# GpSimd strips kept off VectorE's composite passes, the last copy in two tiles, and a new table of turns in an attention and feed-forward kernel

## The chip, the cores and the metric

The kernel runs on one core of a Trainium2 chip. A core has five engines with a queue each: TensorE (PE, with a separate row for its weight loads, PEld), VectorE (DVE), ScalarE (ACT), GpSimd (POOL) and SyncE (SP, here only a queue of DMAs). The metric is the device time of one execution in microseconds (us); the time of a kernel is the median of several executions.

## The reference

Both branches read the same `x` of 2048 rows by 512 columns in bfloat16, and a gate mixes them:

```python
g = _sigmoid((x * gate_w).sum(-1, keepdims=True))
a = _A_ref(x, A_wqkv, A_wo)                    # attention, 32 heads of 16 columns
b = _B_ref(x, B_w_gate, B_w_up, B_w_down)      # (silu(x @ w_gate) * (x @ w_up)) @ w_down, 1792 wide
return g * a + (1 - g) * b
```

In the attention, each head has scores of 2048 by 2048, `softmax(q k / 4)`, times `v`; the heads' results go through `wo`.

## The kernel before

**Tiling.** The attention is cut into 32 *units*: 4 blocks of 512 queries (`QBW`) times 8 groups of 4 heads. A unit has 16 *slots*, one for each block of 128 keys, so there are 512 slots. In a slot TensorE makes the scores of 4 heads, 128 keys by 512 queries each.

**Two ways to the exponential.** Most slots take ScalarE: two heads' scores (`s_t`, 128x1024 in PSUM) go through one `Exp` into `e_t` (`emit_pair`, line 752), two such pairs a slot. The rest take VectorE (`emit_d`, line 830): it reads one head's scores (`d_t`, 128x512) with a multiply and an add into 16-bit integers that stand for the bits of a rough exponential (line 848), four reads to a block of 128x2048, and then makes the value better with *passes* over the whole block (`class Pass`, line 882): either three shifted copies, so that TensorE sums four versions, or two bit masks and a product. `v_unit` (line 1607) decides when a block goes to VectorE, by the time that the plan expects VectorE to be free.

**Strips.** GpSimd helps with the passes (copies and products). `strip` (line 940) gives it the last columns of a pass, as many as fit into a time; `g_now` (line 979) works out this time: from the end of GpSimd's last strip, or 0.1 us after VectorE's last SBUF pass, to the end of the reads of PSUM that VectorE is expected to do next, plus `G_OVER` = 0.05 us (or 0.4 in turns marked `q`). The idea is that GpSimd works while VectorE reads PSUM. `wide(cost)` (line 339) tells which of the small waiting operations count as SBUF passes rather than as reads; it goes by their booked cost, under 0.45 us. Those, and the passes, are booked no earlier than the end of the running strip (`plan.lock`). A strip gets a semaphore on VectorE's last pass (`beside`, line 959).

**The plan.** All engines' queues are written in an order worked out in Python while the kernel is built. `plan` (line 318) holds a clock for each engine, with booked costs: 0.217 us for a matmul of 512 columns, 0.9167 for an exp tile, 0.6 for a read of PSUM and for a full copy pass, 1.135 for a product (`MUL_US`). `fill_dve` (line 1009) picks VectorE's next work; operations with a due time wait in `owed` (`later`, line 348) with a cost and, where given, a key. Where an operation has the key of the one just before it, `spend_v` adds 0.13 us and `fill_dve` looks for another that is due first. `TURNS` (line 87) holds two letters for each pair of score tiles; a letter changes one choice of the plan at that pair (how much slack a piece of work may take, whether a block may start, whether products or copies go to GpSimd, and others), and a dot changes nothing.

**The other work** is cut into pieces that the pacer puts into gaps of TensorE: the projections of q, k and v, the feed-forward chunks (56 of them: `gu_chain`, line 686), the down projections and the output. A chunk has `gate`, whose `Tanh` on ScalarE is followed on VectorE by `gs` (line 701), and `gated`, which multiplies by the up half into `mt` (line 689). `gate_end` (line 646) makes the odds of the gate for all rows at once, five small operations booked at 1.7; `recip` (line 1150) inverts a query block's softmax denominators and spreads them (`rn`, booked at 1.1 or 0.87).

**The end.** The last unit's result `o_ps` is copied to SBUF in two halves, one on VectorE and one on ScalarE (`post`, line 1123), both into one tile `osb`. Then `denominators` (four small matmuls into `dt`), a reciprocal (`rt`), `spread_rows` (16 small matmuls into `rps`), four products (`on_l`), four closing matmuls into `a_ps` (`a_l_a`, `a_l_b`, `al`, `al_o`), four evictions and the stores follow (lines 1757 to 1784). `rest` holds ten products of rows 2 and 3 of the last block that need none of this; `tail(n)` (line 1215) emits n of them.

Of the kernel before, what the change touches and what calls it, by code (L numbers as in the profile page):

```python
# [8 lines left out]
ACT = mybir.ActivationFunctionType  # L9
ALU = mybir.AluOpType  # L10
# [43 lines left out]
class Pacer:  # L54
# [30 lines left out]


TURNS = (
    "....d...sq.t.......q................i......v...........ld..q...........y........................"
    "...........n...............r......e............................................................."
    ".................................l........e.......................j..g...........v...m.....gk..."  # L90
    "..............o.......c...j........n..........h....l.......................t........k...b......."
    "..c.i......q....j.......c......u.........q..............................o......................."
    ".................................x...qh.....k.......................a..n...................u...l"
    "...........x..j.d..x.....x..a...........c.......j.c..wi...iw.................t....jv............"
    ".....t...v..k.c.a..l.rh.......j.h.......e.........on..i...............j......f............c...sy"
    "........kx..............j...............k...s...........................................a......f"
    "..c...................................................................o....uj......x............"
    "..c...d..q.q.....y...uh.d............ra.................k.b......n............i.a..fe..........."
    ".....................................................................................m.......x.q"
    ".......tkq...vb....l.............y..b..u...y.................qe........n...x..e.............e..q"  # L100
    "........b........................vc....l...............g.l..d............f.......y.g..k........q"
    "................................................b..........m..............h....................."
    "........k................n.....ya"
)


# [1 line left out]
def kernel(  # L108
# [13 lines left out]
    P = 128  # L122
# [71 lines left out]
    def act(*args, **kw):  # L194
        ordered(nc.scalar.activation(*args, **kw))  # L195
# [136 lines left out]
    def spend(mode, mms, ready=0.0):  # L332
# [3 lines left out]
        plan.pe = max(plan.pe + (FLIP if mode != plan.mode else 0.0), ready) + (0.226 if mode == "F" else 0.217) * mms  # L336
        plan.mode = mode

    def wide(cost):
        return cost < 0.45  # L340

    def took():
        plan.alone, plan.alone_ins = plan.dve, last_of.get(nc.vector.engine)
# [342 lines left out]
    def gu_chain(i):  # L686

        def gated(up):
            vec.scalar_tensor_tensor(out=mt[:, FS[i][1], :], in0=gs_of.pop(i)[:], scalar=0.5, in1=up[:, :],
                                     op0=ALU.mult, op1=ALU.mult)  # L690
            m_free(up, plan.dve)

        def gate(gp):
            th = work.tile([P, QBW], BF16, tag="th", name="th")
            flush_act(plan.pe + 0.5)
            act(out=th[:], in_=gp[:, :], func=ACT.Tanh, scale=0.5)
            plan.act = max(plan.act, plan.pe + 0.38) + 0.49

            def f():
                gs = work.tile([P, QBW], BF16, tag="gs", name="gs")  # L700
                vec.scalar_tensor_tensor(out=gs[:], in0=th[:], scalar=1.0, in1=gp[:, :], op0=ALU.add, op1=ALU.mult)
                m_free(gp, plan.dve)
                gs_of[i] = gs
            gs_at[i] = plan.act + 0.05
            later(0.6, f, gs_at[i])

        cs = slice(FS[i][0] * QBW, (FS[i][0] + 1) * QBW)
        return [columns(DC, "gu", lambda dc, w=w: w[i][:, dc, :], lambda dc: xT[:, dc, cs], end)
                for w, end in ((w_gate, gate), (w_up, lambda p: later(0.6, lambda: gated(p), max(plan.pe + 0.25, gs_at[i]))))]

    scaled = set()

# [251 lines left out]

    G_FIX, G_COPY, G_PRODUCT = 0.195, 0.00083, 0.00187
    G_LEAST, G_LEAVE = 192, 160
    G_OVER = 0.05
    MASKS = False

    def claim(now):  # L970
# [8 lines left out]
    def g_now(now):  # L979

        while True:
            g = claim(now)
            if g is None:
                return
            start = max(plan.pool, plan.alone + 0.1, g.ready + 0.1, 0.0 if g.c is not None or not g.home else min(c_free) + 0.1)
            t = now
            for ready, cost in sorted([(d[0], 0.6) for d in d_wait] + [(o[0], o[1]) for o in owed if not wide(o[1])]):
                if ready > t + 0.05:
                    break
                t += cost  # L990
            if t == now or not g.strip(start, t + (G_OVER if way_of(pairs[0]) != "q" else 0.4) - start):
                return
# [129 lines left out]

    def post(un):
        qb, g = UNIT[un]
        osbs[un] = osb0[qb] if g == 0 else work.tile([P, QBW], BF16, tag="osb", name="osb")
        if un == 0:
            assert part_scaled
            vec.scalar_tensor_tensor(out=osbs[un][:, :], in0=o_of.pop(un)[:, :], scalar=tiny[:, 0:1], in1=o_part, op0=ALU.add, op1=ALU.add)
        elif un == UNITS - 1:
            o, hw = o_of.pop(un), QBW // 2  # L1130
            vec.tensor_scalar(out=osbs[un][:, 0:hw], in0=o[:, 0:hw], scalar1=tiny[:, 0:1], scalar2=None, op0=ALU.add)
            act(out=osbs[un][:, hw:], in_=o[:, hw:], func=ACT.Identity, bias=tiny[:, 0:1], scale=1.0)
        else:
            vec.tensor_scalar(out=osbs[un][:, :], in0=o_of.pop(un)[:, :], scalar1=tiny[:, 0:1], scalar2=None, op0=ALU.add)

# [14 lines left out]
    def recip(qb, g1, n0):  # L1150

        n = 4 * g1
        dn = work.tile([P, P], BF16, tag="dn", name="dn")
        queue.dma_start(out=dn[0:4 * n, :], in_=dds[qb][0:n, :].rearrange("h (a c) -> (h a) c", c=P))
        full = qb < QB - 1
        if full:
            rd = work.tile([P, QBW], BF16, tag="rd", name="rd")[:, :].bitcast(F32)
            queue.dma_start(out=rd[:, 0:P], in_=odds_rows[0][TQ * qb:TQ * (qb + 1), :].unsqueeze(0).broadcast_to([H, TQ, P]))

        def spread():  # L1160
            rn = work.tile([P, P], BF16, tag="rn", name="rn")
            if full:
                vec.reciprocal(rd[:, P:2 * P], dn[:, :])
                vec.tensor_tensor(out=rn[:, :], in0=rd[:, P:2 * P], in1=rd[:, 0:P], op=ALU.mult)
            else:
                recip16(rn[0:4 * n, :], dn[0:4 * n, :])
            rr = dram.tile([H, QBW], BF16, tag="rr", name="rr")
            queue.dma_start(out=rr[0:n, :].rearrange("h (a c) -> (h a) c", c=P), in_=rn[0:4 * n, :])
            for b in range(g1 // 2):
                queue.dma_start(out=rb[:, b, :],  # L1170
                                  in_=rr[8 * b:8 * b + 8, :].unsqueeze(1).broadcast_to([8, DH, QBW]))
        at.setdefault(n0 + 6, []).append(lambda: later(1.1 if full else 0.87, spread))
        for b in range(g1 // 2):
            def norm(b=b):
                vec.tensor_tensor(out=onc[qb][:, b, :], in0=onc[qb][:, b, :], in1=rb[:, b, :], op=ALU.mult)
                normed.add((qb, b))
            at.setdefault(n0 + 13 + b, []).append(lambda norm=norm: later(0.345, norm))

    def denominators(p, osb):
        for tq in range(TQ):  # L1180
            mm(p[:, 4 * tq:4 * tq + 4], lhsT=osb[:, tq * P:(tq + 1) * P], rhs=sel_t[:, :], start=True, stop=True)

    def spread_rows(p, rt):
        for tq in range(TQ):
# [583 lines left out]
    on_l = work.tile([P, QBW], BF16, tag="rd", name="on_l")  # L1768
    for tq in range(TQ):
        cs = slice(tq * P, (tq + 1) * P)  # L1770
        vec.tensor_tensor(out=on_l[:, cs], in0=osb[:, cs], in1=rps[:, cs], op=ALU.mult)
# [44 lines left out]
```

## Time and profile before

| | before |
|---|---|
| time, median of 3 | 754.49 us (753.93 to 754.78) |
| the profiled execution | 753.96 us |
| its span in the profile | 752.2 us |
| granted TensorE clock | 1.00 |
| VectorE reads of score tiles into `c_t` | 460, mean 679 ns |
| ScalarE exp tiles | 756, mean 1071 ns |
| GpSimd strips of copies within `c_t` | 173, mean 789 ns |

The span is shorter than the time by what lies around the program on the device. The profile names a group of instructions by line, engine, operation, what it writes and reads (`c_t<-d_t`), shape and count; behind the bar stand its busy time, the mean of one and the idle time before them. Lines are those of the helpers through which every operation goes, L192, L195 and L204, so the names of the tiles tell operations apart. In a timeline a row has start, length, engine and instruction; `x3` are three in a row. The reported spans of neighbours on VectorE and ScalarE overlap, so what an operation costs is the distance from its start to the next start.

### The profile page before, as it was taken

To read this page: it belongs to the slowest core of one execution; us is meant where nothing else is said; L and a number is where in the kernel's file an instruction comes from. 1 tells how busy PE (TensorE), PEld (TensorE's weight loads), DVE (VectorE), ACT (ScalarE), POOL (GpSimd) and SP (SyncE) were. 2 spreads that over 40 slices of the span, in tenths; PEclk is the share of its full clock that TensorE was granted. 3 is DMA by queue.
4 is the path that set the end of the run, shared out by engine and by line. 5 is a ranking of instruction groups with operands and counts; after the bars stand their busy time and mean duration, and the time that the engine had idled before them with its cause. 6 is when DMAs were issued, how large, how long until landed. Compare 5 with 4: busy or idle time off the path is not lost.

```text
span 752.2 us, 22877 instructions
## 1 busy us (share of the span) xinstructions
PE 731.6 (97%) x9213; PEld 215.6 (29%) x9213; DVE 728.6 (97%) x1233; ACT 733.4 (98%) x825; POOL 291.9 (39%) x352
## 2 busy tenths in 40 slices
PE   8999999999999999999999999999999999999997
PEld 3322222222222223222222222232222322232222
DVE  7899999999999999999999999999999999999994
ACT  5999999999999999999999999999999999999996
POOL 5125444334335353443532254532423363143430
PEclk9999999999999999999999999999999999999999
DMA  9000303153300013221100130311000232100001
GB/s 227 6 1 16 71 17 67 46 135 75 72 20 13 18 42 81 56 48 30 37 20 26 44 84 21 77 37 44 17 13 26 62 84 55 31 20 12 15 31 36
DMA packets 91027, 34.45 MB, mean 46 GB/s; under 512 B 75488, under 2 KB 90472, under 8 KB 90920
## 3 DMA queue, kind: packets, MB, share of 16 engines
q1 hardware_dynamic: 89192, 32.66, 18.1%
q8 instruction: 72, 1.18, 0.6%
q10 hardware_dynamic: 1728, 0.33, 0.2%
q14 instruction: 35, 0.29, 0.1%
HBM read 21.55 MB, written 2.35 MB: 32 GB/s over the span
## 4 chain that ended last, share of the span: by engine, by line
PE 57%; DVE 22%; ACT 14%; issue 5%; POOL 1%; DMA 0%; DVEq 0%; ACTq 0%; POOLq 0%
PE s_t L192 19%; PE o_ps L192 17%; DVE c_t L204 14%; ACT e_t L195 13%; PE gu L192 7%; PE ops L192 5%; PE qp L192 2%; PE kp L192 2%; PE vp L192 2%; DVE mt L204 2%; DVE kaug L204 2%; ACT th L195 1%; DVE gs L204 1%; DVE osb L204 1%; PE dps L192 1%
## 5 line engine op out<-in xcount | busy, mean ns | idle before, releaser
L195 ACT ACTIVATE e_t<-s_t 128x1024 bf16<-128x1024 f32 x756 | 707.7, 1071 | 4.5 <-PE d_t L192 1.7
L204 DVE TENSOR_SCALAR c_t<-d_t 128x512 uint16<-128x512 f32 x460 | 299.7, 679 | 2.1 <-PE d_t L192 1.8
L192 PE MATMUL s_t<-qx,kaug 32*128 32x512 bf16 (+1 forms) x1192 | 231.7, 384 | 7.6 <-ACT e_t L195 6.7
L204 POOL TENSOR_SCALAR c_t<-c_t 128x416 uint16<-128x416 uint16 (+19 forms) x173 | 136.6, 789 | 208.4 <-DVE c_t L204 154.8
L192 PEld LDWEIGHTS <-kaug 32*128 32x128 bf16 (+1 forms) x2048 | 79.3, 91 | 304.9 <-issue 301.6
L192 PE MATMUL d_t<-qx,kaug 32*128 32x512 bf16 x440 | 151.7, 383 | 0.6 <-DVE qx L204 0.3
L192 PE MATMUL o_ps<-e_t,vaug 128*32 128x512 bf16 (+2 forms) x1568 | 148.0, 378 | 0.0
L192 PE MATMUL o_ps<-c_t,vaug 128*32 128x512 bf16 (+2 forms) x1392 | 123.3, 372 | 1.4 <-POOL c_t L204 0.8
L204 DVE TENSOR_SCALAR c_t<-c_t 128x2048 uint16<-128x2048 uint16 (+3 forms) x187 | 121.8, 662 | 0.3
L204 POOL TENSOR_TENSOR c_t<-c_t 128x480 bf16<-128x480 bf16 (+13 forms) x60 | 65.2, 1103 | 131.9 <-DVE c_t L204 84.5
L192 PEld LDWEIGHTS <-vaug 128*32 128x32 bf16 x3216 | 70.5, 95 | 113.2 <-issue 100.6
L192 PE MATMUL gu<-xT,wg 128*32 128x512 bf16 x896 | 72.3, 383 | 0.4 <-DVE mt L204 0.2
L192 PE MATMUL gu<-xT,wu 128*32 128x512 bf16 x896 | 68.3, 382 | 0.3
L192 PE MATMUL ops<-wd_t,mt 128*32 128x512 bf16 x672 | 57.0, 382 | 0.0
L204 DVE TENSOR_TENSOR c_t<-c_t 128x2048 bf16<-128x2048 bf16 (+15 forms) x57 | 56.9, 998 | 0.0
L204 DVE TENSOR_SCALAR kaug<-d_t 128x512 uint16<-128x512 f32 x72 | 47.0, 680 | 0.6 <-PE d_t L192 0.6
L204 DVE SCALAR_TENSOR_TENSOR mt<-gs,gu 128x512 bf16<-128x512 bf16 x56 | 38.0, 679 | 1.6
L204 DVE SCALAR_TENSOR_TENSOR gs<-th,gu 128x512 bf16<-128x512 bf16 x56 | 37.8, 675 | 0.1
L192 PE MATMUL s_t<-q,kaug 32*128 32x512 bf16 (+1 forms) x188 | 36.6, 385 | 1.1 <-ACT e_t L195 0.9
L195 ACT ACTIVATE th<-gu 128x512 bf16<-128x512 f32 x56 | 35.8, 639 | 0.0
L204 POOL TENSOR_SCALAR kaug<-c_t 128x416 uint16<-128x416 uint16 (+15 forms) x34 | 26.8, 788 | 22.2 <-DVE c_t L204 20.0
L204 POOL TENSOR_SCALAR c_t<-kaug 128x1120 uint16<-128x1120 uint16 (+8 forms) x33 | 24.8, 753 | 23.1 <-DVE c_t L204 13.8
(149 smaller groups left out, 548.6 us busy)
## 6 DMA issues: line engine op xcount, KB each, us to landing
wg<-in_B_w_gate_dram SPq DMA_DIRECT2D x56, 128.0 KB
wu<-in_B_w_up_dram SPq DMA_DIRECT2D x56, 128.0 KB
on<-osb SPq DMA_DIRECT2D x120, 16.0 KB
rb<-rr SPq DMA_DIRECT2D x15, 128.0 KB
wd_t<-in_B_w_down_dram SPq DMA_DIRECT2D x7, 256.0 KB
qx<-qst SPq DMA_DIRECT2D x96, 16.0 KB
qx<-aq SPq DMA_DIRECT2D x96, 16.0 KB
out_dram<-o_t SPq DMA_DIRECT2D x12, 128.0 KB
```

What stands on the lines that cost most here:

```text
L192: return ordered(nc.tensor.matmul(*args, **kw))
L195: ordered(nc.scalar.activation(*args, **kw))
L204: return lambda *a, **kw: ordered(f(*a, **kw))
```

## The change

Seven edits in one:

- `wide` also holds for operations booked at 0.87, 1.4 or 1.7 us: the odds (`gate_end`) and the spread of reciprocals (`recip`), whose full form is now booked at 1.4 rather than 1.1. They are so kept from strips like the passes.
- `G_OVER` goes from 0.05 to 0: a strip ends, by the plan, with the last read. A strip behind another is booked to start 0.08 us after it.
- `gs` and the `mt` product of one chunk share a key.
- The two halves of the last copy get a tile each; `block` finds the columns of a row block in either form.
- The ten last products are put 3, 3, 2 and 2 instead of 2, 2 and 6, the last two between the second and the third closing matmul.
- In the evictions at the end, ScalarE takes the first and third, VectorE the second and fourth.
- `TURNS` is replaced: 150 letters before, 131 after, at other places.

```diff
 TURNS = (
-    "....d...sq.t.......q................i......v...........ld..q...........y........................"
...
+    "..........s...j.....d........................r.......................q....b...s......l.........l"
...
 )
+    PASSES = (0.87, 1.4, 1.7)
+
     def wide(cost):
-        return cost < 0.45
+        return cost < 0.45 or cost in PASSES
...
-            later(0.6, f, gs_at[i])
+            later(0.6, f, gs_at[i], ("g", i))
...
-                for w, end in ((w_gate, gate), (w_up, lambda p: later(0.6, lambda: gated(p), max(plan.pe + 0.25, gs_at[i]))))]
+                for w, end in ((w_gate, gate), (w_up, lambda p: later(0.6, lambda: gated(p), max(plan.pe + 0.25, gs_at[i]), ("g", i))))]
...
-    G_OVER = 0.05
+    G_OVER = 0.0
...
-            start = max(plan.pool, plan.alone + 0.1, g.ready + 0.1, 0.0 if g.c is not None or not g.home else min(c_free) + 0.1)
+            start = max(plan.pool + 0.08, plan.alone + 0.1, g.ready + 0.1, 0.0 if g.c is not None or not g.home else min(c_free) + 0.1)
...
-        osbs[un] = osb0[qb] if g == 0 else work.tile([P, QBW], BF16, tag="osb", name="osb")
+        if un < UNITS - 1:
+            osbs[un] = osb0[qb] if g == 0 else work.tile([P, QBW], BF16, tag="osb", name="osb")
...
-            vec.tensor_scalar(out=osbs[un][:, 0:hw], in0=o[:, 0:hw], scalar1=tiny[:, 0:1], scalar2=None, op0=ALU.add)
-            act(out=osbs[un][:, hw:], in_=o[:, hw:], func=ACT.Identity, bias=tiny[:, 0:1], scale=1.0)
+            osbs[un] = [work.tile([P, hw], BF16, tag=t, name="osb")[:, :] for t in ("osb", "th")]
+            vec.tensor_scalar(out=osbs[un][0], in0=o[:, 0:hw], scalar1=tiny[:, 0:1], scalar2=None, op0=ALU.add)
+            act(out=osbs[un][1], in_=o[:, hw:], func=ACT.Identity, bias=tiny[:, 0:1], scale=1.0)
...
-        at.setdefault(n0 + 6, []).append(lambda: later(1.1 if full else 0.87, spread))
+        at.setdefault(n0 + 6, []).append(lambda: later(1.4 if full else 0.87, spread))
...
+    def block(osb, tq):
+        if isinstance(osb, list):
+            osb, tq = osb[tq // 2], tq % 2
+        return osb[:, tq * P:(tq + 1) * P]
...
-    tail(min(2, len(rest)))
+    tail(min(3, len(rest)))
     dt = m_tile("dt")
     denominators(dt, osb)
...
-    tail(min(2, len(rest)))
+    tail(min(3, len(rest)))
...
     spread_rows(rps, rt)
-    tail(len(rest))
+    tail(min(2, len(rest)))
...
     for tq in range(TQ):
+        if tq == 2:
+            tail(len(rest))
         mm(a_ps[tq][:, 0:D], lhsT=on_l[:, tq * P:(tq + 1) * P], rhs=wo_l[:, 1, :], start=False, stop=True,
...
-        if tq % 2 == 0:
+        if tq % 2:
             vec.tensor_scalar(out=mt[:, tq, :], in0=a_ps[tq][:, 0:D], scalar1=gval[:, t:t + 1], scalar2=None, op0=ALU.mult)
```

More of the change, by code (lines that the diff above doesn't have):

```diff
@@ L87 @@
 TURNS = (
-    "....d...sq.t.......q................i......v...........ld..q...........y........................"
[L89 to L102, printed above, removed]
@@ L103 @@
-    "........k................n.....ya"
+    "..........s...j.....d........................r.......................q....b...s......l.........l"
+    ".....n.y...f.x....a...b.................k........t............k...h........x...........g....a.s."
+    ".......................t..................k...................o................................."
+    "...r......k....................n...................q.....g................k..............r.m...."
+    ".........w....................hq..........h...................o......y....d..n..k.....h........."
@@ new lines @@
+    "..hqj....xkt.y............a.c.....k....x....c.................................s...........o...j."
+    ".......t....j.......i....x......c.s.......e.............j......................................."
+    ".....q........................b..f......k.a...b....................................l............"
+    "..............o...................................s............................................."
+    "..........s........................r..............................................i.........j..."
@@ new lines @@
+    "..i............r..............................i............................r.....v........b....."
+    ".....q...g..c...b.........h......n...ye..q...q...lc........w............a....w......iq.........."
+    "..........b....................n..if.......t....c.............................d..............q.."
+    "...............f.......v....h......u....k..m..cxk........v..................................e..."
+    "...f..........j....q..................................o............w............kg.............."
@@ L104 @@
+    ".......g..................o"
 )
@@ L1177, in recip @@
             at.setdefault(n0 + 13 + b, []).append(lambda norm=norm: later(0.345, norm))
+    def block(osb, tq):
+        if isinstance(osb, list):
+            osb, tq = osb[tq // 2], tq % 2
+        return osb[:, tq * P:(tq + 1) * P]
     def denominators(p, osb):
         for tq in range(TQ):
-            mm(p[:, 4 * tq:4 * tq + 4], lhsT=osb[:, tq * P:(tq + 1) * P], rhs=sel_t[:, :], start=True, stop=True)
+            mm(p[:, 4 * tq:4 * tq + 4], lhsT=block(osb, tq), rhs=sel_t[:, :], start=True, stop=True)
     def spread_rows(p, rt):
@@ L1770 @@
         cs = slice(tq * P, (tq + 1) * P)
-        vec.tensor_tensor(out=on_l[:, cs], in0=osb[:, cs], in1=rps[:, cs], op=ALU.mult)
+        vec.tensor_tensor(out=on_l[:, cs], in0=block(osb, tq), in1=rps[:, cs], op=ALU.mult)
     for tq in range(TQ):
+        if tq == 2:
+            tail(len(rest))
         mm(a_ps[tq][:, 0:D], lhsT=on_l[:, tq * P:(tq + 1) * P], rhs=wo_l[:, 1, :], start=False, stop=True,
```

## The prediction

> **What bounds the kernel now.** I read the page first, busy time and the slices.
>
> ```profile
> span 752.2 us, 22877 instructions
> PE 731.6 (97%) x9213; PEld 215.6 (29%) x9213; DVE 728.6 (97%) x1233; ACT 733.4 (98%) x825; POOL 291.9 (39%) x352
> PE   8999999999999999999999999999999999999997
> DVE  7899999999999999999999999999999999999994
> ACT  5999999999999999999999999999999999999996
> ```
>
> Three engines are full together from the second slice to the last but one. Such a kernel is bounded by whichever of them falls behind the order that the program wrote down for all three. The table by stages shows where there is room:
>
> ```profile
> 300.00:400.00 100.00, 98.31 (x1238) 28.38 (x1230) 99.55 (x164) 99.55 (x113) 41.58 (x52) 1.00 0.16 38
> 740.00:753.00 13.00, 7.69 (x81) 2.69 (x80) 3.79 (x9) 4.97 (x7) 0.00 (x0) 0.99 0.16 52
> ```
>
> In a middle stage VectorE and ScalarE are both at 99.55 of 100 us; only the last 13 us are a chain in which engines take turns. Then the groups:
>
> ```profile
> L195 ACT ACTIVATE e_t<-s_t 128x1024 bf16<-128x1024 f32 x756 | 707.7, 1071 | 4.5 <-PE d_t L192 1.7
> L204 DVE TENSOR_SCALAR c_t<-d_t 128x512 uint16<-128x512 f32 x460 | 299.7, 679 | 2.1 <-PE d_t L192 1.8
> L204 DVE TENSOR_SCALAR c_t<-c_t 128x2048 uint16<-128x2048 uint16 x165 | 114.0, 698 | 0.3
> L204 POOL TENSOR_SCALAR c_t<-c_t 128x1120 uint16<-128x1120 uint16 x21 | 23.6, 1124 | 67.3 <-DVE c_t L204 63.1 <-PE gu L192 1.7 <-DVE kaug L204 1.6
> L204 POOL TENSOR_TENSOR c_t<-c_t 128x224 bf16<-128x224 bf16 x13 | 7.9, 614 | 0.0
> ```
>
> ScalarE takes 756 exp tiles in 707.7 us, 0.936 us a tile. Spans of neighbours overlap, so the spacing of starts counts: a lone tile has 1.06 us, and two in a row where nothing waits have 1.95 (both rows stand below), a spacing of 0.89. About 0.03 to 0.05 us a tile, over 20 us in all, is therefore late feeding that a busy share does not show. VectorE has no such room: reads of PSUM start every 0.60 us though each is reported as 0.68. **VectorE is what falls behind; ScalarE is fed late because of it.** Here is one such place:
>
> ```profile
> 278.49 0.69 DVE L204 TENSOR_SCALAR c_t<-c_t 128x2048 uint16<-128x2048 uint16 x1
> 279.09 0.94 DVE L204 RECIPROCAL rd<-dn 128x128 f32<-128x128 bf16 x1
> 280.07 1.04 DVE L204 TENSOR_TENSOR rn<-rd 128x128 bf16<-128x128 f32 x1
> 281.03 0.67 DVE L204 SCALAR_TENSOR_TENSOR gs<-th,gu 128x512 bf16<-128x512 bf16 x1
> ...
> 279.32 2.76 POOL L204 TENSOR_TENSOR c_t<-c_t 128x768 bf16<-128x768 bf16 x3 [2.83 <-DVE c_t L204]
> ...
> 598.57 0.29 DVE L204 TENSOR_TENSOR rn<-rd 128x128 bf16<-128x128 f32 x1
> ```
>
> The same `rn` product takes 0.29 us at 598.57, where GpSimd is idle, and 1.04 at 280.07 under a strip. ScalarE just behind it:
>
> ```profile
> 278.08 1.06 ACT L195 ACTIVATE e_t<-s_t 128x1024 bf16<-128x1024 f32 x1
> 279.46 2.92 ACT L195 ACTIVATE e_t<-s_t 128x1024 bf16<-128x1024 f32 x3
> 282.58 2.14 ACT L195 ACTIVATE e_t<-s_t 128x1024 bf16<-128x1024 f32 x2 [0.20 <-PE s_t L192]
> 285.10 1.95 ACT L195 ACTIVATE e_t<-s_t 128x1024 bf16<-128x1024 f32 x2
> ```
>
> Three tiles starting 0.9 apart from 279.46 would hand over at 282.15; the next starts at 282.58, and its pair has a spacing of 1.08 (2.14 less 1.06) instead of 0.89. That is 0.43 and 0.19, together 0.6 us of the 0.75 that the product lost. So a VectorE loss arrives at ScalarE at about four fifths, through the written order of TensorE.
>
> **The change, part by part.** The sum is made against the profiled execution's own 753.96 us (span 752.2 and 1.8 around it), 0.5 below the median of 754.49; I add the 0.5 at the end.
>
> *Passes freed of strips.* The odds (1.7) and the spread of reciprocals (1.4 and 0.87) now count as passes: no strip is laid over them, they wait for one that runs.
>
> ```profile
> 440.70 0.98 DVE L204 TENSOR_TENSOR rn<-rd 128x128 bf16<-128x128 f32 x1
> 172.32 0.96 DVE L204 TENSOR_TENSOR omg<-ge,gval 128x16 f32<-128x16 f32 x1
> 616.71 1.05 DVE L204 TENSOR_TENSOR on<-on,rb 128x512 bf16<-128x512 bf16 x1
> ```
>
> Two `rn` products give back 1.04 and 0.98 less 0.29 each, 1.4 us; `omg`, smaller than `rn`, at least 0.96 less 0.29, 0.7 us. The `on` product was a pass already and lies under a strip that began late; I count nothing for it. The reciprocal itself is 0.94 under the strip, so I count nothing there either. Together **-2.1** of VectorE. The new wait is short: behind a pass that waits for a strip stand the next reads on VectorE, but the order takes due reads first, and a strip behind a pass waits for its end on GpSimd, which idles 61% of the span.
>
> *Strips that end with the reads.* A strip was allowed 0.05 us past the last read and the next was booked with no gap; now 0 and 0.08. What the overhang costs:
>
> ```profile
> 132.90 0.68 DVE L204 TENSOR_SCALAR c_t<-c_t 128x2048 uint16<-128x2048 uint16 x1
> 304.49 0.83 DVE L204 TENSOR_SCALAR c_t<-c_t 128x2048 uint16<-128x2048 uint16 x1
> L204 DVE TENSOR_SCALAR c_t<-kaug 128x2048 uint16<-128x2048 uint16 x30 | 20.8, 705 | 0.1
> ```
>
> A full copy pass is 0.68 alone (132.90) and 0.83 under a strip's end (304.49). The means of 698 over 165 and 705 over 30 lie 16 and 23 ns over 682: 3.3 us in all. The overhang is not the only reason why a strip is late (its start waits for a semaphore), so I take half: **-1.7**, with 0 and -3.3 as ends.
>
> Against it stands what the shorter strips leave to VectorE. The strips, 327 by the groups, lose 0.05 us each where they begin a run and 0.08 behind another: about 0.065, 21 us of GpSimd. A strip of 1120 columns is 1.12 us of GpSimd and 1120/2048 of 0.60, 0.33 us, of VectorE: 0.3 to 1. So up to **+6.3** of VectorE; below, 0, because strips that end with their pass, or by the rounding to 32 columns, lose nothing. I take +5, near the upper end, since most widths above are cut by time. The strips of 224 columns (0.61 us) are the ones that no longer fit at all: 0.52 us leave under the least of 192 columns.
>
> *gs and mt of one chunk get a common key*, which books 0.13 us where they follow each other and takes another read in between if one is due.
>
> ```profile
> 134.09 0.67 DVE L204 SCALAR_TENSOR_TENSOR gs<-th,gu 128x512 bf16<-128x512 bf16 x1
> 134.87 0.69 DVE L204 SCALAR_TENSOR_TENSOR mt<-gs,gu 128x512 bf16<-128x512 bf16 x1
> ...
> 631.79 0.67 DVE L204 SCALAR_TENSOR_TENSOR gs<-th,gu 128x512 bf16<-128x512 bf16 x1
> 632.57 0.69 DVE L204 SCALAR_TENSOR_TENSOR mt<-gs,gu 128x512 bf16<-128x512 bf16 x1
> ```
>
> The second starts 0.78 behind the first, not 0.60: 0.18 us lost, at 15 of 56 chunks (first and last shown). I expect 12 of them to be parted, **-2.1**; ends 0 and -2.7.
>
> *The end of the kernel.* The chain of the last 10 us, in the timeline:
>
> ```profile
> 743.75 0.48 DVE L204 TENSOR_SCALAR osb<-o_ps,tiny 128x256 bf16<-128x256 f32 x1 [0.33 <-PE o_ps L192]
> 744.26 0.47 ACT L195 ACTIVATE osb<-o_ps,tiny 128x256 bf16<-128x256 f32 x1 [1.03 <-DVE osb L204]
> 745.03 0.26 DVE L204 RECIPROCAL rt<-dt 128x16 bf16<-128x16 f32 x1 [0.80 <-PE dt L192]
> 747.02 0.38 PE L192 MATMUL a_l_a<-wo_l,on_l 128*128 128x512 bf16 x1
> 747.67 0.38 PE L192 MATMUL al_o<-wo_l,on_l 128*128 128x512 bf16 x1
> 748.11 0.74 DVE L204 TENSOR_SCALAR mt<-al,gval 128x512 bf16<-128x512 f32 x1
> 748.24 0.68 ACT L195 ACTIVATE mt<-al_o,gval 128x512 bf16<-128x512 f32 x1
> ```
>
> Both halves of the last copy lie in one tile, and ScalarE waited 1.03 us for VectorE's half. In two tiles both start at 743.75: the denominators end 0.5 earlier, the reciprocal starts at 744.53. Three products (0.22 each, the spacing of the four from 747.02 to 747.67) before and three behind it put the spread at 745.15; two more, and `a_l_a` starts at 745.95 instead of 747.02. The last two products now stand between the second and third closing matmul: `al` at 746.8, `al_o` at 747.03 (before 747.67). Evictions then run alternately and the last ends near 748.2 instead of 748.92. Queued behind the added wait for a matmul are only the evictions themselves. **-0.7**; ends -0.3 and -1.0. The last store is issued behind it as before.
>
> *The table anew.* It moves pieces of work between slots; no row can price it. What it can change is the number of key blocks that VectorE takes. A block is two exp tiles (2 x 0.936, 1.9 us of ScalarE) or four reads (2.4) and its passes on VectorE, about 4.4 us with strips (reads of all tiles 349 us and passes some 240, over 134 blocks). So extra VectorE work that the plan sees is shared: of 1 us, 1.9/(1.9+4.4), 0.3 us, arrives at the end, in steps of a block.
>
> *The sum.* Losses that the plan did not know vanish: 2.1, 1.7 and 2.1 are 5.9, which arrive at three quarters: -4.4. The +5 is known to the new plan: 0.3 of it is 1.5, rounded up to one block more for ScalarE: +1.9. With -0.7 at the end: -3.2, so 750.8 for the execution profiled, **751.3** as a median.
>
> A rule of the Trainium skill speaks against the third term: VectorE: DVE Perf Modes, section "The DRAIN you can't avoid", says that the next operation does not start until the pipe has emptied, whatever stands between. By it nothing is won by parting gs from mt. The rows above differ: reads start 0.60 us apart though each is reported at 0.68, and only the pair has 0.78; no row of before shows all chunks parted.
>
> **The rivals.**
>
> *Same.* VectorE is full, so what is handed back (5 to 6.3) cancels what is freed (5.9), with no block moved: only the end is left, 753.8; it spans 753.0 to 755.5. For it: both numbers come out alike. Against: the freed part is lateness against the order, the other is booked. 0.20. That strips still lie over passes because a semaphore makes them later than booked belongs here: it takes away the 1.7 and leaves 752.6 to 754.
>
> *Slower.* Strips too short: if over 18 us of GpSimd time goes and the new table finds no order for it, 6.3 us of VectorE arrive whole; with half of the freed 5.9 this is +6.3 - 3.0 - 0.7, 757.1. It decides where GpSimd's busy time falls from 292 to under 274 with exp tiles at 756 or more. For it: products of 224 columns drop out. 0.17.
>
> *Faster by more.* The table also wins a block or two for VectorE, 754 tiles or fewer on ScalarE: 1.9 less each and the +1.9 not paid: 747.5 to 749.4. 0.18.
>
> *The parting is worth nothing.* If 0.18 us is a flush that moves with the operation, 2.1 times three quarters is missing: 752.9. The named section would have it so. 0.05.
>
> **How the numbers follow.** Forecast (749.6 to 752.9) 0.40, faster by more 0.18, nothing from parting 0.05, same 0.20, slower 0.17. A measurement here tells about 0.2%, 1.5 us, from no change: below 753.0 is faster, above 756.0 slower. Faster 0.40 + 0.18 + 0.04 = 0.62; slower 0.16 (the rival's lower edge lies within 0.2%); the rest, 0.22, is same. The range leaves out half of each outer case: 748.0 to 757.0.
>
> **What would show it.** Right: `rn` three times at 0.3 us; copy passes of full width with a mean near 685; gs and mt seldom 0.78 apart; GpSimd's busy time down by 10 to 20 us; 756 to 758 exp tiles at a spacing nearer 0.92; both halves of the last copy starting together. Wrong: exp tiles at 752 or 762; tiles that still need 0.936 us each although the passes are clean, for then VectorE's losses were not what fed ScalarE late; or an `o_ps` matmul that waits for GpSimd.

## The result and the profile after

| | before | after |
|---|---|---|
| time, median of 5 | 754.56 us (753.93 to 754.85) | 748.07 us (747.60 to 748.27) |
| ratio, 95% interval | | 0.9913 (0.9898 to 0.9927) |
| span of the profiled execution | 752.2 us | 746.2 us |
| exp tiles on ScalarE | 756 | 756 |
| GpSimd busy | 291.9 us | 278.5 us |

The kernel is 6.5 us faster. The forecast was 751.3, 3.2 us faster; the direction holds, and the measured time lies at the lower end of the range of 748.0 to 757.0; the size is twice the forecast.

The page of after, busy time and slices:

```profile
span 746.2 us, 22814 instructions
PE 725.7 (97%) x9173; PEld 214.7 (29%) x9173; DVE 724.0 (97%) x1242; ACT 730.5 (98%) x825; POOL 278.5 (37%) x348
PE   8999999999999999999999999999999999999997
DVE  7899999999999999999999999999999999999995
ACT  5999999999999999999999999999999999999996
```

It looks as before: three engines full, none freed. Their busy times fell with the span, which fits a kernel whose engines all wait a little less for one of them but does not say for which. The groups that answer to those of before:

```profile
L195 ACT ACTIVATE e_t<-s_t 128x1024 bf16<-128x1024 f32 x756 | 707.1, 1094 | 1.9 <-PE s_t L192 1.1
L204 DVE TENSOR_SCALAR c_t<-d_t 128x512 uint16<-128x512 f32 x472 | 309.0, 683 | 2.4 <-PE d_t L192 1.9
```

The exp tiles are 756 again, so VectorE has 134 key blocks as before (the reads, 472 into `c_t` here and 64 into the two other homes, are 536 in both). No work moved between ScalarE and VectorE. By shape, VectorE's full copy passes and GpSimd's costliest groups:

```profile
L204 DVE TENSOR_SCALAR c_t<-c_t 128x2048 uint16<-128x2048 uint16 x158 | 107.0, 685 | 0.5
L204 DVE TENSOR_SCALAR c_t<-kaug 128x2048 uint16<-128x2048 uint16 x25 | 17.0, 685 | 0.1
...
L204 POOL TENSOR_SCALAR c_t<-c_t 128x1088 uint16<-128x1088 uint16 x42 | 46.1, 1097 | 90.5 <-DVE c_t L204 66.5 <-DVE kaug L204 9.1 <-PE o_ps L192 5.1
L204 POOL TENSOR_TENSOR c_t<-c_t 128x480 bf16<-128x480 bf16 x38 | 41.5, 1095 | 105.4 <-DVE c_t L204 57.4 <-DVE kaug L204 26.7 <-PE d_t L192 11.7
L204 POOL TENSOR_SCALAR c_t<-c_t 128x352 uint16<-128x352 uint16 x41 | 19.8, 483 | 68.5 <-DVE c_t L204 50.8 <-DVE kaug L204 11.5 <-DVE rn L204 3.4
```

The full passes have a mean of 685 ns where they had 698 and 705: the overhang is nearly gone. The commonest strips of copies are narrower (1088 and 352 columns, where 1120 and 416 were the widths), as the edit says. The places of the prediction, in the timeline of after:

```profile
282.31 0.94 DVE L204 RECIPROCAL rd<-dn 128x128 f32<-128x128 bf16 x1
283.28 0.29 DVE L204 TENSOR_TENSOR rn<-rd 128x128 bf16<-128x128 f32 x1
283.49 0.68 DVE L204 SCALAR_TENSOR_TENSOR gs<-th,gu 128x512 bf16<-128x512 bf16 x1
284.08 0.68 DVE L204 TENSOR_SCALAR c_t<-d_t 128x512 uint16<-128x512 f32 x1
284.69 0.68 DVE L204 SCALAR_TENSOR_TENSOR mt<-gs,gu 128x512 bf16<-128x512 bf16 x1
...
283.65 1.10 POOL L204 TENSOR_TENSOR c_t<-c_t 128x480 bf16<-128x480 bf16 x1 [1.22 <-DVE rn L204]
...
169.86 0.18 DVE L204 TENSOR_TENSOR omg<-ge,gval 128x16 f32<-128x16 f32 x1
```

`rn` takes 0.29 us (1.04 before) and the next strip waits for it; a read stands between `gs` and `mt`; `omg` takes 0.18 (0.96). In the whole trace 3 pairs of `gs` and `mt` still follow each other, of 15. And the end:

```profile
738.14 0.48 DVE L204 TENSOR_SCALAR osb<-o_ps,tiny 128x256 bf16<-128x256 f32 x1 [3.29 <-PE o_ps L192]
738.66 0.47 ACT L195 ACTIVATE osb<-o_ps,tiny 128x256 bf16<-128x256 f32 x1 [1.00 <-DVE osb L204]
740.79 0.39 PE L192 MATMUL a_l_a<-wo_l,on_l 128*128 128x512 bf16 x1
741.88 0.38 PE L192 MATMUL al_o<-wo_l,on_l 128*128 128x512 bf16 x1
742.08 0.69 ACT L195 ACTIVATE mt<-al,gval 128x512 bf16<-128x512 f32 x1 [0.18 <-PE al L192]
742.30 0.75 DVE L204 TENSOR_SCALAR mt<-al_o,gval 128x512 bf16<-128x512 f32 x1
```

The two tiles do not do what was expected of them: ScalarE's half still waits for VectorE's. The last eviction ends 4.91 us behind the start of the copy, where it was 5.17 in the kernel before.

**Where the 6 us of span went.** I added up the distances from each VectorE start to the next, by kind, from 20 us after the start to 8 us before the start of the last exp tile, idle time apart:

```
us of VectorE             before   after   difference
copies and masks           149.4   151.0     +1.6
products                    66.8    64.8     -2.0
odds and spreads             7.6     5.3     -2.3
on products                  5.8     5.1     -0.7
gs and mt                   68.1    67.2     -0.9
reads of d_t               322.4   322.1     -0.3
all other                   86.4    85.6     -0.8
idle                         6.8     6.9     +0.1
all                        713.4   708.0     -5.4
```

The last exp tile ends at 743.2 before and 737.7 after, 5.6 earlier. The stretch ends with that tile, so the totals must differ by about as much, whatever the cause; what the table shows is that the difference lies in the distances of VectorE's operations and not in its idle time, and in which kinds. Of the 0.18 us that `mt` loses behind its `gs`, 0.10 is reported as idle time and stands in that row: with it the parted pairs are worth 2.2 us, and idle time elsewhere rose by 1.3.

The exp tiles' lateness (what the distances between two in a row exceed 0.904 us, their median before) fell from 19.3 to 13.9 us, 5.4 as well; the mean distance fell from 0.931 to 0.924. The busy time does not show it: 707.1 us are 0.935 a tile where the prediction read 0.936, and it had called that a sign of being wrong. The reported spans grew instead, from a mean of 1071 to 1094 ns.

The row of copies and masks hides two changes that nearly cancel. The plan books a copy at 0.066 us and 0.534 for each 2048 columns, a product at 0.066 and 1.069 (`strip`). I set these prices beside the distances, over the whole kernel:

```
us of VectorE                   before     after
copies and masks, columns      492,960   515,488
  at the plan's prices          145.83    152.16
  by distances                  151.75    153.49
products, columns              118,432   115,168
  at the plan's prices           66.77     65.20
  by distances                   68.03     65.58
```

VectorE was handed 4.8 us of work (6.3 of copies more, 1.6 of products less). What its passes lose over the plan's prices fell from 7.2 us to 1.7 (copies 5.9 to 1.3, products 1.3 to 0.4), 5.5 us. On GpSimd, copies fell from 192.8 to 167.7 us and products rose from 89.8 to 101.1.

### The profile page after: what moved, and what is told of

It reads as the page before. It is cut to its first block, busy times and chain, and to the rows that moved or that the text cites. A ratio compares the mean times of both kernels' runs of the same rounds, so it can differ in the third digit from the quotient of the medians.

```text
span 746.2 us, 22814 instructions
## 1 busy us (share of the span) xinstructions
PE 725.7 (97%) x9173; PEld 214.7 (29%) x9173; DVE 724.0 (97%) x1242; ACT 730.5 (98%) x825; POOL 278.5 (37%) x348
## 4 chain that ended last, share of the span: by engine, by line
PE 54%; ACT 27%; DVE 12%; issue 7%; DMA 0%; ACTq 0%; DVEq 0%
ACT e_t L195 25%; PE s_t L192 18%; PE o_ps L192 15%; DVE c_t L204 7%; PE gu L192 6%; PE ops L192 5%; PE dps L192 2%; ACT th L195 2%; PE qp L192 2%; PE kp L192 2%; PE vp L192 2%; DVE mt L204 1%; DVE kaug L204 1%; DVE gs L204 1%; PE warm L192 1%
## 5 line engine op out<-in xcount | busy, mean ns | idle before, releaser
L195 ACT ACTIVATE e_t<-s_t 128x1024 bf16<-128x1024 f32 x756 | 707.1, 1094 | 1.9 <-PE s_t L192 1.1
L204 DVE TENSOR_SCALAR c_t<-d_t 128x512 uint16<-128x512 f32 x472 | 309.0, 683 | 2.4 <-PE d_t L192 1.9
L204 POOL TENSOR_SCALAR c_t<-c_t 128x1088 uint16<-128x1088 uint16 (+14 forms) x203 | 147.8, 728 | 206.2 <-DVE c_t L204 147.6
L192 PE MATMUL d_t<-qx,kaug 32*128 32x512 bf16 x444 | 145.3, 384 | 0.0
L204 DVE TENSOR_SCALAR c_t<-c_t 128x2048 uint16<-128x2048 uint16 (+7 forms) x181 | 114.8, 646 | 0.5
L204 POOL TENSOR_TENSOR c_t<-c_t 128x480 bf16<-128x480 bf16 (+7 forms) x55 | 61.5, 1128 | 141.3 <-DVE c_t L204 93.3
L192 PEld LDWEIGHTS <-vaug 128*32 128x32 bf16 x3176 | 66.9, 95 | 108.5 <-issue 95.1
L204 DVE TENSOR_TENSOR c_t<-c_t 128x1568 bf16<-128x1568 bf16 (+10 forms) x51 | 47.8, 938 | 0.0
L204 DVE TENSOR_SCALAR kaug<-d_t 128x512 uint16<-128x512 f32 x52 | 34.7, 682 | 0.5 <-PE d_t L192 0.5
L204 DVE TENSOR_SCALAR kaug<-c_t 128x2048 uint16<-128x2048 uint16 (+5 forms) x50 | 33.5, 669 | 0.1
L192 PEld LDWEIGHTS <-mt 128*32 128x32 bf16 (+1 forms) x1037 | 24.4, 95 | 26.9 <-issue 20.1
```

The costliest lines, as they stand in the source:

```text
L192: return ordered(nc.tensor.matmul(*args, **kw))
L204: return lambda *a, **kw: ordered(f(*a, **kw))
```

## The experiments

Theory V: VectorE's starts set the time of the middle; the rules (all edits but the table and the end) free it of losses that its plan did not know. Theory T: the new table's order is the gain. Ratios are to the kernel before on the same chip.

**The end alone.** Before, with the edits of the end only (lines 1123 to 1132, `block`, and lines 1756 to 1784).

> The kernel before with only the edits of the end: two tiles for the last copy, products 3, 3, 2 and 2, evictions exchanged; plan and table as before. Theory V (VectorE's chain of starts sets the time of the middle, the end is a small part): the trace of after shows the two halves of the copy still one behind the other, and the last eviction 4.91 us behind the start of the copy instead of 5.17, so 0.3 to 0.4 us come from the end: 754.1. The prediction's own step would give 0.7: 753.8. Rival E (the end is a large part of the 6.5 us): 752 or less.

753.60 us, ratio 0.9993 (0.9984 to 1.0001). About 0.5 us, not clear of nothing; the trace's last eviction is 0.3 earlier against the start of the copy, as in after. The end is a small part.

**Rules and table apart.**

```diff
 TURNS = (        # old_table: after with the table of before
                  # new_table: before with the table of after
                  # blank_before, blank_after: both with an empty table
```

> The kernel after with the table of before. Theory V (the rules free VectorE of losses that were not booked, and the table only trims): most of the gain stays, 748 to 750.5, with rn at 0.3 us, full copy passes at a mean near 685 ns and few of the gs and mt pairs 0.78 apart. Rival T (the new table is the gain): 752 to 755, although the passes are as clean.

> The kernel before with the table of after. Theory V: the losses are back, so about the time of before, 753 to 757 (the table was not made for these rules), rn near 1 us where a strip lies over it. Rival T: 749 to 751.

> The kernel before with an empty table. Ground on which the rules can be compared without a table made for either of them. Theory V: slower than before by what a table is worth, 757 to 770.

> The kernel after with an empty table. Theory V (the rules are the gain): below the kernel before with an empty table by 3 to 8 us. Rival T (the table is the gain): within 2 us of it, or above it, since the shorter strips hand work back to VectorE.

| rules | own table | empty table | the other's table |
|---|---|---|---|
| before | 754.56 | 758.40 (1.0050, 1.0035 to 1.0065) | 762.97 (1.0116, 1.0100 to 1.0132) |
| after | 748.07 (0.9913) | 756.95 (1.0031, 1.0019 to 1.0043) | 757.79 (1.0047, 1.0035 to 1.0060) |

Both theories missed. I expected `old_table` to keep most of the gain, and it is 3.7 us slower than before; `new_table` was expected at 753 to 757 and is 8.9 slower. Each of the two tables beats an empty one under its own rules, by 3.8 and 8.9 us, and is no faster than the empty one under the other's (0.8 us slower, within the intervals, and 4.6). What the misfit does stands on the pages, `old_table`, then `new_table`, then `blank_after`:

```profile
PE 730.0 (97%) x9208; PEld 218.0 (29%) x9209; DVE 720.7 (95%) x1223; ACT 739.4 (98%) x835; POOL 205.6 (27%) x263
```

```profile
PE 733.5 (96%) x9200; PEld 218.5 (29%) x9201; DVE 719.2 (94%) x1209; ACT 742.2 (97%) x837; POOL 218.9 (29%) x261
```

```profile
PE 730.8 (97%) x9208; PEld 218.2 (29%) x9209; DVE 719.0 (95%) x1229; ACT 739.4 (98%) x835; POOL 211.9 (28%) x286
```

GpSimd works 206 to 219 us instead of 279 to 292, and ScalarE has 835 or 837 instructions instead of 825: ten exp tiles or twelve, five or six key blocks that VectorE did not get. In the same sums as above VectorE is idle 17 to 25 us in these kernels, 7 with a table of its own. So a fitting table goes with a plan in which VectorE has few holes and GpSimd takes strips; both tables reach the same 756 tiles, one for each set of rules. On equal empty ground the rules gain only 1.5 us (758.40 to 756.95), where theory V expected 3 to 8. What passes lose over the plan's prices goes with the rules, not with the table: for copies it is 5.9, 5.5 and 5.9 us under the old rules (own, other and empty table) and 1.3, 2.8 and 2.1 under the new.

**Half the table.** After with the first 8 lines of its table, 768 characters or 384 pairs (the expectation says 720 and 360).

> The kernel after with the first 720 characters of its table (360 pairs of 756), the rest empty. If letters work where they stand, the kernel keeps its lead over the empty table (749 + 8.9 at the end) up to the middle, 5 to 6 us at unit 16, and then runs as with the empty table: 750.5 to 752.5, with 760 to 762 exp tiles. If the table only works as a whole: 755 to 758.

752.15 us (0.9969, 0.9958 to 0.9981), 760 exp tiles. By VectorE's copies of `o_ps` its units close within 0.4 us of those of after up to unit 17, and the last closes 3.8 later. Letters act where they stand.

**What arrives of a VectorE loss.** Twelve reductions of which the plan knows nothing are put on VectorE, one at the close of every second unit.

```diff
             post(un)
+            if un in range(3, 27, 2):
+                vec.tensor_reduce(out=extra[:, :], in_=xT[:, 0, 0:QBW], axis=AX.X, op=ALU.max, apply_absolute_value=True)
```

> The kernel after with 12 more VectorE operations (a reduction of 128x512, about 0.55 to 0.6 us each, 6.8 us in all), one at the close of every second unit from 3 to 25, of which the plan knows nothing; the order of all other work is the same. Theory V: they arrive whole, 748.1 + 6.8 = 754.9. The prediction's own step (three quarters): 753.2. Rival A (ScalarE or TensorE sets the time and VectorE has room): under 750.5.

> The kernel before with the same 12 operations at the close of the same units. Theory V: 754.5 + 6.8 = 761.3. Three quarters: 759.6. Rival A: under 757.

After with them: 754.89 us, ratio 1.0004 (0.9994 to 1.0013); against 0.9913 that is 6.9 us. Before with them: 760.50, 1.0076 (1.0060 to 1.0093), 5.7 us, less than the expected 6.8. The group in the trace of the first:

```profile
L204 DVE TENSOR_REDUCE extra<-xT 128x1 f32<-128x512 bf16 x12 | 8.1, 676 | 0.0
```

Less the 0.08 by which reported spans overlap, 12 of 0.60 are 7.2 us; 0.95 and 0.8 of it arrive. The order of all other work was the same, so nothing but VectorE's lateness can have done it. This holds for V and against a kernel in which ScalarE or TensorE sets the time and VectorE has room. Nothing was added to ScalarE or TensorE, so the runs do not show that lateness there would arrive less.

**The strips over rn and omg put back.**

```diff
+    def cover(cols):                      # waits for VectorE's last operation
+        ins = gps.tensor_tensor(out=shade[:, 0:cols], in0=xT[:, 0, 0:cols], in1=xT[:, 1, 0:cols], op=ALU.mult)
...
+                cover(800)                # ahead of each spread's reciprocal; 544 ahead of the odds
                 vec.reciprocal(rd[:, P:2 * P], dn[:, :])
```

> The kernel after with a product of two stretches of xT on GpSimd, into a scratch tile, started over each of the three spreads (800 columns) and over the odds (544 columns); the plan knows nothing of it and the order of all other work is the same. It puts back the strips that lay over rn and omg in before. Theory V: rn 0.29 to about 1.0 three times and omg to about 0.9, 0.7 to 0.8 us each, which arrive whole: 748.1 + 2.9 = 751.0. Rival R (the table's order is the gain and such waits are absorbed): 748.1 to 748.8.

750.17 us (0.9945, 0.9932 to 0.9957): 2.1 us above after, 2.4 by the ratios, where 2.9 were expected. The timeline:

```profile
282.92 0.94 DVE L204 RECIPROCAL rd<-dn 128x128 f32<-128x128 bf16 x1
283.89 1.04 DVE L204 TENSOR_TENSOR rn<-rd 128x128 bf16<-128x128 f32 x1
284.85 0.67 DVE L204 SCALAR_TENSOR_TENSOR gs<-th,gu 128x512 bf16<-128x512 bf16 x1
...
283.07 1.71 POOL L204 TENSOR_TENSOR shade<-xT 128x800 bf16<-128x800 bf16 x1
```

`rn` is at 1.04 or 1.03 again, three times, and here ends 0.15 us behind the strip; `omg` is at 0.93. The reciprocal just before it, 0.94, is not slowed.

**The length of strips alone**, at a fixed order: the plan books the strip as ever, and GpSimd gets other columns.

```diff
-            beside(self.run(gps, slice(self.left - w, self.left)))
+            more = w + (64 if self.home else 32)      # strips_shorter, on before: -64, -32
+            if w == self.left:                        # a strip that ends its pass takes what is left
+                more = self.real
...
+            beside(self.run(gps, slice(self.real - more, self.real)))
+            self.real -= more                         # VectorE's pass ends at self.real
```

> The kernel after with each strip 64 columns (copies) or 32 columns (products) longer than the plan has it, about 0.05 us, and VectorE's part shorter by them; plan, order and table unchanged. It is the old overhang alone. Theory V by its sums: VectorE saves 233 x 64 and 90 x 32 columns, 4.3 and 1.5 us, and pays the overhang, 4 to 5 us of longer passes as in before: net between -2 and +1, 746 to 749. Rival B (ending the strips with the reads is itself the gain): 751 or more. Rival C (columns count, overhang does not): 742.5.

> The kernel before with each strip 64 or 32 columns shorter than its plan has it, VectorE's part longer by them; plan, order and table of before. The edit of the strips alone, at a fixed order. Theory V: 246 x 64 and 81 x 32 columns go to VectorE, +4.6 and +1.4 us, and the overhang's 4 to 5 us go: net 0 to +2, 754 to 757. Rival B: 750 or less.

`strips_longer` 749.08 (0.9928, 0.9915 to 0.9940), about 1.1 above after; `strips_shorter` 753.31 (0.9984, 0.9975 to 0.9993), 1.2 below before. Both are on the same side: shorter strips are a small gain by themselves. The second is clear of no change; the interval of the first overlaps that of after. I had expected a small loss in the second. The passes of the two, first `strips_shorter`, then `strips_longer`:

```profile
L204 DVE TENSOR_SCALAR c_t<-c_t 128x2048 uint16<-128x2048 uint16 x165 | 112.3, 688 | 0.3
```

```profile
L204 DVE TENSOR_SCALAR c_t<-c_t 128x2048 uint16<-128x2048 uint16 x158 | 107.8, 689 | 0.5
```

698 to 688, and 685 to 689. The columns handed over are far fewer than a count of strips gives: VectorE's copies gained 4,224 columns in `strips_shorter` (497,184 where before has 492,960), not 246 x 64 = 15,744, because the strip that ends a pass takes what is left. What passes lose over the plan's prices fell from 7.2 to 4.2 us in `strips_shorter` and rose from 1.7 to 5.1 in `strips_longer`: the length of the strips sets most of it.

**The third edit alone.** Before, with `mt` made from the `gs` of the chunk before.

```diff
-            vec.scalar_tensor_tensor(out=mt[:, FS[i][1], :], in0=gs_of.pop(i)[:], scalar=0.5, in1=up[:, :],
+            vec.scalar_tensor_tensor(out=mt[:, FS[i][1], :], in0=gs_all[max(i - 1, 0)][:], scalar=0.5, in1=up[:, :],
```

> The kernel before with the product into mt reading the gs of the chunk before (a stale factor; its own gs is left out), so that it does not depend on the operation just ahead of it; order, plan and table of before. Theory V: the 15 pairs 0.78 apart become 0.60 apart, 2.7 us of VectorE, of which 0.8 to 0.95 arrive: 752.0 to 752.4 where before has 754.5. If the 0.18 us is a flush of the engine that any two such operations pay, the pairs stay at 0.78 and the time at 754.5.

752.17 us (0.9974, 0.9963 to 0.9984): 2.0 us by the ratio. The first pair:

```profile
134.23 0.67 DVE L204 SCALAR_TENSOR_TENSOR gs<-th,gu 128x512 bf16<-128x512 bf16 x1
134.82 0.68 DVE L204 SCALAR_TENSOR_TENSOR mt<-gs,gu 128x512 bf16<-128x512 bf16 x1
```

0.59 apart, still neighbours, and 13 of the 15 pairs are at 0.59 to 0.60 (the other two at 0.66 and 0.70): the 0.18 us came with the dependence, not with the operation.

**Losses taken away, at the order of before.** The edits of the end, the shorter strips and the stale `gs` together on before, and the products `rn` and `omg` replaced by reciprocals that leave out their second factor:

```diff
-                vec.reciprocal(rd[:, P:2 * P], dn[:, :])
-                vec.tensor_tensor(out=rn[:, :], in0=rd[:, P:2 * P], in1=rd[:, 0:P], op=ALU.mult)
+                recip16(rn[:, :], dn[:, :])
...
-            vec.tensor_tensor(out=omg[:, :], in0=ge[:, :], in1=gval[:, :], op=ALU.mult)
+            vec.reciprocal(omg[:, :], gval[:, :])
```

> The kernel before, its rules, table and order kept, with its unbooked losses taken away one by one: the edits of the end, strips 64 or 32 columns shorter, the stale gs, and the two products under strips replaced by reciprocals, which strips do not slow (rn and omg are left without their second factor; that also saves 0.6 us of work). Theory V: 0.5 + 1.1 + 2.4 + 2.5 = 6.5 us: 748.0, the time of after without its table. Rival T (the new order itself is worth some of the 6.5): 750.5 or more.

748.94 us (0.9934, 0.9921 to 0.9946), 5.0 us below before, where theory V expected 6.5 and theory T at most 4. Its page shows the matmuls of before (9213) and a busy time near after's:

```profile
PE 726.2 (97%) x9213; PEld 215.2 (29%) x9213; DVE 725.4 (97%) x1230; ACT 731.3 (98%) x825; POOL 282.2 (38%) x352
```

The last exp tile ends at 738.0, 5.3 us earlier than before and 0.3 later than after. So 5.0 us come without a new table and, but for the end, without a new order; 0.6 of them are work left out, and the wait is gone at all 15 pairs where after parts 12. It is not the same set of losses as in after: copies still lose 4.5 us over the plan's prices. The rest of the 6.5, 1.5 us, is about what the two intervals leave open (0.9921 to 0.9946 against 0.9898 to 0.9927).

**The last copy.** `one_copy` is after with the whole copy on VectorE; `act_first` is after with ScalarE's half written first.

```diff
-            vec.tensor_scalar(out=osbs[un][0], in0=o[:, 0:hw], scalar1=tiny[:, 0:1], scalar2=None, op0=ALU.add)
             act(out=osbs[un][1], in_=o[:, hw:], func=ACT.Identity, bias=tiny[:, 0:1], scale=1.0)
+            vec.tensor_scalar(out=osbs[un][0], in0=o[:, 0:hw], scalar1=tiny[:, 0:1], scalar2=None, op0=ALU.add)
```

> The kernel after, with the last unit's copy made whole on VectorE in one tile. In the trace of after ScalarE's half starts when VectorE's half has ended (1.00 us of waiting, released by that copy), so the two take 0.48 and 0.47 in a row. If two readers of this tile always go one behind the other, a whole copy, about 0.74 as reported, ends 0.2 to 0.3 us earlier: 747.8. If the two tiles do help at some other place, it is 748.1 or more.

> The kernel after with ScalarE's half of the last copy written ahead of VectorE's. If the program orders any two readers of this PSUM tile, VectorE's half now starts when ScalarE's ends, about 0.5 us behind it. If only ScalarE's half is held for another reason, both start together and the end comes 0.5 us earlier.

```profile
738.39 0.47 ACT L195 ACTIVATE osb<-o_ps,tiny 128x256 bf16<-128x256 f32 x1 [0.48 <-PE o_ps L192]
...
738.90 0.48 DVE L204 TENSOR_SCALAR osb<-o_ps,tiny 128x256 bf16<-128x256 f32 x1 [3.79 <-ACT osb L195]
```

Now VectorE's half waits for ScalarE's. Whichever reader of the tile `o_ps` comes second in the program waits for the first; separate targets do not change that, and no run here shows why. `one_copy` has 748.03 us (0.9920, 0.9908 to 0.9933), the same as after; in its trace `a_l_a` starts 2.47 us behind the copy (740.59 less 738.12) instead of 2.65. No kernel here beats after by more than its interval.

## Why the prediction was right in direction and wrong in size

**Right: what bounds the kernel.** Losses of VectorE reach the end through TensorE's order; `after_unbooked` and `before_unbooked` show it. The prediction let three quarters arrive, from one place; the runs give 0.95 and 0.8. On 5.9 us that is 0.3 to 1.2 us too little.

**Wrong: the overhang, "so I take half: -1.7, with 0 and -3.3 as ends".** This is the step that failed. The term was read from the reported means of the full-width copies alone, and no row stood behind the half. By distances, VectorE's passes freed 5.5 us, beyond even the far end: the operation behind a full copy started 0.620 us after it on average and now 0.605, and passes of part width and products gained too. At a fixed order, longer strips alone bring 3.4 of it back.

**Wrong: "+5 is known to the new plan ... rounded up to one block more for ScalarE: +1.9".** The +5 itself was well sized: 4.8 us of work were handed to VectorE. But it was not shared. The exp tiles are 756 in both kernels, no block moved, and the 4.8 stand on VectorE whole. This error goes the other way, for 4.8 is more than 1.9, so it does not explain why the kernel is faster than forecast. GpSimd's busy time is no measure of it: 21 us were counted and the page has 13.4, because copies fell by 25.0 and products rose by 11.3.

**The sum with the measured sizes.** Freed are 2.3 (odds and spreads), 5.5 (overhang), 2.2 (`gs` and `mt`) and 0.7 (`on`), 10.7 us where the prediction had 5.9. Less the 4.8 handed back that is 5.9; smaller pieces on both sides leave the 5.4 of the table. The table of turns was counted at nothing beyond a block's step, while an empty one costs the new rules 8.9 us: it is what keeps the 756 tiles. The two wrong terms pulled against each other; that the measured time still lies just inside the range is luck.

**The other terms.** Passes freed: -2.1 forecast, -2.3 by distances; 2.1 to 2.4 us come back in the time when three `rn` and the `omg` are covered again. The `on` product, counted at nothing, gave 0.7. Parting `gs` from `mt`: -2.1 forecast for 12 pairs; 12 were parted, 2.2 by distances, and freeing all 15 of the wait gave 2.0. The rule that the prediction cites from the Trainium skill (VectorE: DVE Perf Modes, section "The DRAIN you can't avoid") would have made this nothing. The runs do not bear it out: neighbours without a dependence start 0.59 apart. The same section adds "A next op that is not held starts earlier", which the prediction left out.

**The end: -0.7 forecast, 0.3 by the trace, 0.5 by the time and not clear of nothing.** The step "in two tiles both start at 743.75" is false. What did come is from the products and evictions moved: `a_l_a` starts 2.65 us behind the copy instead of 3.27, of which 0.26 is left at the last eviction.

**Rivals.** "Same" had the handed-back work right, whole and with no block moved, but it set 5.9 us of freed time against it instead of 10.7. "Slower" named as its sign a GpSimd busy time under 274 us; it is 278.5. "Faster by more", which holds the measured 748.07, came, but not by its mechanism, more blocks for VectorE. What stays open is how much of the last 1.5 us is the new order, what the 0.08 us booked between two strips does by itself, and what a table fitted as well to the old rules as this one is to the new would have given.

## What to carry to other kernels

When three engines are each 97% busy and one order binds them, look for starts that lie further apart than the plan books: a few tenths of a microsecond in a few dozen places arrive at the end nearly whole (here 0.8 to 0.95 of them). Price such a loss by the distances between starts of every operation that can have it, not by the mean span of one group: the mean gave 3.3 us here, the distances 5.5. Compare schedules only when each has choices fitted to it; a rule tried under a table made for another rule is measured with the misfit, here 9 to 10 us against the rule's own table, more than the rule is worth. Before work handed to another engine is priced by the number of its instructions, look at which of them are cut by time and which by the end of the work.

## What the runs showed of the hardware

- A product of two SBUF tensors on VectorE under a GpSimd strip waits for the strip's end (1.04 us where it takes 0.29 alone, ending 0.15 behind the strip, `covered`). This is as the Trainium skill has it (SBUF — State Buffer, section "Who interferes with whom"): with two SBUF inputs it contends with a GpSimd instruction that reads SBUF, and the second of the two to issue blocks until the first has finished. The reciprocal under the same strip kept its 0.94.
- The product `mt`, which reads the `gs` written just before it, starts 0.78 us behind it (15 pairs in before); reading an older `gs`, it starts 0.59 to 0.60 behind it in 13 of the same 15 places (`gs_stale`, 128x512).
- Longer GpSimd strips beside the same passes of VectorE cost these passes time: with 64 or 32 columns more a strip at the same order, they lose 3.4 us more over the plan's prices, in all (`strips_longer`).
